# Attention and maxout layer on one core: K and Q through the crossbar one slot earlier, stores held back, queries read in natural order

## The chip, the cores and the metric

The kernel runs on one core of a Trainium2 chip. The metric is the device time of one execution in microseconds (us). Five engines work side by side, each through its own instructions in order: TensorE (PE, with its weight loads shown apart as PEld), VectorE (DVE), ScalarE (ACT), GpSimd (POOL) and SyncE (SP), which here only issues DMA transfers. SP, ACT and POOL each have a queue that can issue DMAs.

## The reference

Sliding-window attention with four sink positions, and on its result a feed-forward layer that takes the largest of three products:

```python
batch, n_heads, seq, head_dim = (4, 8, 768, 64);  n_sink, window = (4, 128)
scores = (1.0 / np.sqrt(D)) * np.matmul(q, k.transpose(0, 1, 3, 2))
keep = (pos[None, :] < n_sink) | ((rel >= 0) & (rel < window))     # rel = query - key
scores = np.where(keep, scores, -1000000000.0)
a = np.exp(scores - max);  a = a / sum(a)
x = np.matmul(a, v).transpose(0, 2, 1, 3).reshape(B * S, H * D)    # 3072 x 512
h = np.maximum(np.maximum(x @ w1, x @ w2), x @ w3)                 # 3072 x 768
out = (h @ w_out).astype(np.float32)                               # 3072 x 512
```

All inputs and the output are float32.

## The kernel before

**Tiling.** The 3072 rows are cut into 12 chunks of 256 rows (`ci`), three for each of the four sequences. A chunk is two blocks of 128 queries. Heads go in four pairs (`p`): the two heads of a pair lie on the two halves of the 128 partitions of the transposed Q and K. The matmuls run in bf16.

**The stages of a chunk.** `load` (L74) brings K, Q and V from DRAM as float32, 512 KB each (L78), with two neighbouring rows on one partition, so that each descriptor moves 512 bytes. Row 2r + i of a block lies on partition r, place i. `cast` (L488) makes bf16 copies of K and Q (`cast_qk`, L173) and of V (`cast_v`, L180), mostly on POOL. K and Q are then transposed so that the head dimension lies on the partitions: in chunks 0 and 1 by float32 matmuls against an identity (`turn32`, L193), in chunks below `KQ_XBAR` = 4 by PE transposes (`turn`, L205), from chunk 4 on by the DMA crossbar on SP (`turn_xbar`, L214: two transposes for K at L217, one for Q at L220). `sink_score` (L248) and `score` (L261) multiply (PE, L254 and L279) and take the exponential (ACT, L258 and L281). `mask` (L283) multiplies by a 0/1 mask on DVE. `av` (L293) multiplies by V, with a column of ones for the sum, and divides on DVE into `x`. `x` is transposed to `xT`: by PE (`xpose`, L328) below `X_XBAR` = 4, by two crossbar transposes on SP (`xpose_xbar`, L337, L339) from chunk 4 on. `ffn_h` (L346) makes one of nine groups of h (eight matmuls of 256 columns, L352): the first of three products is copied by ACT (L356), the two others are taken in by a max on DVE (L358). `F(ci, n)` (L501) is the n-th such group. `ffn_y` (L360) makes one block of y (six matmuls of 512 columns, L363), copies it on ACT (L369) and stores it by two DMAs of 64 rows on SP (L371).

**Permuted queries.** K, Q and V are read from DRAM as "(p i)", so after the transposes the columns are in the order i, r (all even rows, then all odd rows). The score matmuls read Q in that order (`q_ap`, L244). So x, h and y of a block are in the order i, r as well, and the store puts them back with a view of the output as "(r i) f -> i r f", one DMA for each i.

**What sets the order.** The schedule is written out by hand: `manual_schedule` keeps each engine's instructions in program order, and waits are put in where a tile is written or read. Chunks 0 to 3 are written out one by one (L384 to L572), with weight loads on POOL (`load_w`, L144, casting in the DMA) and two loads held back by small writes of POOL into their buffer (`gate`, L69). From chunk 4 on a loop runs (L574 to L594), one slot for each chunk i: `attend(i + 1)` (av and the transposes of x), `cast(i + 2)`, the load of chunk i + 3, four F groups of chunk i, `turn_xbar(i + 2)`, `scores(i + 2)`, the two y blocks of chunk i - 1 with masks between them, and the other five F groups. SP's queue in a slot is then: two transposes of x (i + 1), three loads (i + 3), three transposes of K and Q (i + 2), four stores of y (i - 1).

**Buffers.** Raw loads 3 deep, bf16 K and Q 2, transposed K 4 and Q 3 (`kT`, `qT`, L109), V with ones 4 (`vb`, L111), x, xT and h 3, y 4, exponentials 10, PSUM 8 banks in one rotation (`bank`, L58).

Of the kernel before, what the change touches and what calls it, by code (L numbers as in the profile page):

```python
# [14 lines left out]
def kernel(  # L15
# [17 lines left out]

    nc = tc.nc
# [14 lines left out]
    KQ_XBAR = 4  # L49
    X_XBAR = 4  # L50

    with tc.manual_schedule():
# [21 lines left out]
        def load(ci, parts):  # L74
            b, c = divmod(ci, CPB)
            for t, g in parts:
                h = slice(0, H) if g is None else slice(4 * g, 4 * g + 4)
                nc.sync.dma_start(  # L78
                    out=raws[ci][t][:, h],
                    in_=dram[t][b, h, c * 256:c * 256 + 256].rearrange("h (p i) d -> p h (i d)", i=2))  # L80

        HALVES = [("k", 0), ("q", 0), ("k", 1), ("q", 1), ("v", 0), ("v", 1)]
        for ci in (0, 1):
            load_begin(ci)
            load(ci, HALVES)

# [12 lines left out]
        for i in range(2):  # L99
# [3 lines left out]
                base=-i, pattern=[[1, 2], [2, 64]], channel_multiplier=-2)  # L103
            nc.gpsimd.affine_select(
                out=msk0[ip, 0, 1], in_=msk0[ip, 0, 1], compare_op=ALU.is_gt, fill=0.0,
                base=i, pattern=[[-1, 2], [-2, 64]], channel_multiplier=2)
# [4 lines left out]
        vb = [const.tile([128, 2, H, D + 1], BF16, name=f"vb{s}") for s in range(4)]  # L111
# [17 lines left out]
        def consts_late(eng):  # L129
            for s in range(1, 4):  # L130
                eng.memset(vb[s][:, :, :, D:D + 1], 1.0)
# [48 lines left out]
        def cast_v(ci, n, i, eng):  # L180
            eng.tensor_copy(vb[ci % 4][64 * i:64 * i + 64, n, :, 0:D],  # L181
                            raws[ci]["v"][64 * n:64 * n + 64, :, i])
# [49 lines left out]
        def sink_v(b, eng):  # L232
            t = bank([128, 2, D + 1], F32, "vs_ps")
            for p in range(NP):
                for h in range(2):
                    nc.tensor.matmul(t[32 * p:32 * p + 32, h], lhsT=sel[:, h],
                                     rhs=vb[(CPB * b) % 4][:, 0, 2 * p + h],
# [6 lines left out]
        def q_ap(ci, p, n):  # L244
            x = qT[ci % 3][:, p].rearrange("p i n r -> p n i r")
            return x if n is None else x[:, n]

        def sink_score(ci):  # L248
# [3 lines left out]
            st = bank([128, 2, 2, 64], F32, "sk")  # L252
# [5 lines left out]
            nc.scalar.activation(e, st.rearrange("p n i r -> p n (i r)"), AF.Exp, scale=scale)  # L258
            es[ci, "sink"] = e

        def score(ci, p):  # L261
# [5 lines left out]
            for what in range(lo, 4):  # L267
                if what == 2:
                    continue
                for h in range(2):  # L270
# [4 lines left out]
                    if what == 1:  # L275
                        o = o.rearrange("p n (i r) -> p n i r", r=64)
                    else:
                        o = o.rearrange("p (i r) -> p i r", r=64)
# [14 lines left out]
        def av(ci, pairs, eng=None):  # L293
# [10 lines left out]
            for p in pairs:  # L304
                first = c == 0
                for t in range(2):
                    for s, n in ((2 * t, 2 * c + t - 1), (2 * t + 1, 2 * c + t)):
                        if n < 0:
                            continue
                        for h in range(2):  # L310
                            nc.tensor.matmul(  # L311
                                o[p][:, t, h], lhsT=es[ci, p][:, h, s],
                                rhs=vb[(CPB * b + n // 2) % 4][:, n % 2, 2 * p + h],
# [9 lines left out]
        def xT_of(ci):  # L323
            if ci not in xTs:
                xTs[ci] = work.tile([128, DS, 256], BF16, tag="xT", name="xT")
            return xTs[ci]

        def xpose(ci, g, eng):  # L328
            pt = bank([128, 2, 2, 128], BF16, "xt_ps")
            x = xs[ci].rearrange("p t h d -> p t (h d)")  # L330
            for a in range(2):
                for t in range(2):
                    ds = 2 * g + a
                    nc.tensor.transpose(pt[:, a, t], x[:, t, ds * 128:(ds + 1) * 128], ident)
            eng(xT_of(ci)[:, 2 * g:2 * g + 2], pt.rearrange("p a t c -> p a (t c)"))  # L335

        def xpose_xbar(ci):  # L337
            for t in range(2):
                nc.sync.dma_start_transpose(  # L339
                    out=xT_of(ci)[:, :, t * 128:(t + 1) * 128],  # L340
                    in_=xs[ci][:, t].rearrange("p h d -> p (h d)"))
# [4 lines left out]
        def ffn_h(ci, wi, fp):  # L346
# [3 lines left out]
            for f in range(2):  # L350
                for ds in range(DS):
                    nc.tensor.matmul(hp[:, f], lhsT=w_sb[wi, 2 * fp + f][:, ds],  # L352
                                     rhs=xTs[ci][:, ds], start=(ds == 0), stop=(ds == DS - 1))
# [5 lines left out]

        def ffn_y(ci, t, last=False):  # L360
# [4 lines left out]
            y = work.tile([128, d_model], F32, tag="y", bufs=4, name="y_sb")  # L365
            r0 = ci * 256 + t * 128
            o = out[r0:r0 + 128].rearrange("(r i) f -> i r f", i=2)
            if not last:
                nc.scalar.copy(y, yp)  # L369
                for i in range(2):  # L370
                    nc.sync.dma_start(out=o[i], in_=y[64 * i:64 * i + 64])  # L371
                return
            for i in range(2):
                ip = slice(64 * i, 64 * i + 64)
                if i:
                    nc.vector.tensor_copy(y[ip], yp[ip])
                else:
                    nc.scalar.copy(y[ip], yp[ip])
                (nc.sync, nc.scalar)[i].dma_start(out=o[i], in_=y[ip])

        V, P, A = nc.vector, nc.gpsimd, nc.scalar


        consts_dve()  # L384
        warm(8)
        turn32(0, "k", 0, V.tensor_copy)
        turn32(0, "q", 0, A.copy)
        warm(2)
        score(0, 0)
        turn32(0, "k", 1, V.tensor_copy)  # L390
        score(0, 1)
        turn32(0, "q", 1, A.copy)
        for n in range(2):
            for i in range(2):
                cast_v(0, n, i, P)
        mask(0, 0, V)
        score(0, 2)
        mask(0, 1, V)
        wait_for(raws[1]["k"][0:1, 0, 0, 0:1], P)
        load_w(0, 0, 256)  # L400
        load_w(0, 256, 256)
        load_w(0, 512, 256)
        load_w(1, 0, 256)
        turn32(1, "k", 0, V.tensor_copy)
        score(0, 3)
        turn32(1, "q", 0, V.tensor_copy)
        av(0, [0])
        mask(0, 2, V)
        av(0, [1])
        xpose(0, 0, A.copy)  # L410
        mask(0, 3, V)
        av(0, [2])
        turn32(1, "k", 1, V.tensor_copy)
        av(0, [3])
        turn32(1, "q", 1, V.tensor_copy)
        score(1, 0)
# [10 lines left out]
        mask(1, 0, V)  # L427
        ffn_h(0, 0, 0)
        score(1, 1)
        mask(1, 1, V)  # L430
# [4 lines left out]
        mask(1, 2, V)  # L435
# [3 lines left out]
        mask(1, 3, V)  # L439
        ffn_h(0, 1, 0)  # L440
        av(1, [2, 3])
        ffn_h(0, 1, 1)
        xpose(1, 0, A.copy)
        xpose(1, 1, A.copy)
        ffn_h(0, 1, 2)

        load_begin(2)
        wait_for(wts[2, 0][0:1, 0, 0:1], P)
        gate(2, "kqv", P)
        load(2, [("k", None), ("q", None), ("v", None)])  # L450
        for a in range(2):
            load_wo(a)
        for fp in range(3):
            ffn_h(1, 0, fp)
        cast_qk(2, "k", 0, P)
        cast_qk(2, "k", 1, P)
        for fp in range(3):
            ffn_h(1, 1, fp)
        for i in range(2):
            for n in range(2):  # L460
                cast_v(2, n, i, P)
        ffn_h(0, 2, 0)
        ffn_h(0, 2, 1)
        ffn_h(0, 2, 2)
# [170 lines left out]
```

## Time and profile before

| what | us |
|---|---|
| median of 3 runs (lowest, highest) | 271.96 (270.34, 273.59) |
| the profiled execution | 271.53 |
| its span, first to last instruction | 269.6 |
| one period of the loop, by the chain | 25 to 27 |
| mean granted clock of TensorE | 0.870 of full |

How to read it: the page has the busy time of each engine, the span in 40 slices (a digit is the busy share in tenths; PEclk is the clock that TensorE was granted), and the chain of work that ended last, followed back from the end. A line "A <- B: total, times, longest" in the waits says how long A stood still until B was done. Further lines of the page, the groups of DMA issues with their size and the median time from issue to landing:

```profile
out_dram<-y_sb SPq DMA_DIRECT2D x47, 128.0 KB, 2.4
k_raw<-in_k_dram SPq DMA_DIRECT2D x10, 512.0 KB, 4.6
q_raw<-in_q_dram SPq DMA_DIRECT2D x10, 512.0 KB, 5.8
v_raw<-in_v_dram SPq DMA_DIRECT2D x10, 512.0 KB, 7.1
```

### The profile page before, as it was taken

To read this page: it belongs to the slowest core of one execution; us is meant where nothing else is said; L and a number is where in the kernel's file an instruction comes from. 1 tells how busy PE (TensorE), PEld (TensorE's weight loads), DVE (VectorE), ACT (ScalarE), POOL (GpSimd) and SP (SyncE) were. 2 spreads that over 40 slices of the span, in tenths; PEclk is the share of its full clock that TensorE was granted. 3 is DMA by queue.
4 is the path that set the end of the run, shared out by engine and by line. 5 is a ranking of instruction groups with operands and counts; after the bars stand their busy time and mean duration, and the time that the engine had idled before them with its cause. 6 is when DMAs were issued, how large, how long until landed. Compare 5 with 4: busy or idle time off the path is not lost.

```text
span 269.6 us, 4874 instructions
## 1 busy us (share of the span) xinstructions
PE 186.8 (69%) x1934; PEld 138.2 (51%) x1946; DVE 115.1 (43%) x251; ACT 90.8 (34%) x177; POOL 64.3 (24%) x130
## 2 busy tenths in 40 slices
PE   6878999987777605940894099219903990999992
PEld 5665786774565503830483058115802580587870
DVE  4385676458186502640273028113800380283441
ACT  1528308453727105210711081015202510812221
POOL 3592223647351033005200510070015000000000
PEclk9999999999999965995599579757975798699998
DMA  6999974999892293339033903692187116034133
GB/s 185 278 147 189 199 178 122 251 264 245 216 232 43 47 254 50 80 67 282 4 78 82 270 2 78 162 190 48 38 197 148 45 40 113 0 80 93 26 78 79
DMA packets 71750, 34.92 MB, mean 130 GB/s; under 512 B 27440, under 2 KB 68656, under 8 KB 71728
## 3 DMA queue, kind: packets, MB, share of 16 engines
q1 hardware_dynamic: 67152, 31.34, 52.3%
q0 software_dynamic: 4496, 3.15, 8.1%
q8 instruction: 15, 0.25, 0.4%
q10 hardware_dynamic: 80, 0.13, 0.2%
q14 instruction: 7, 0.06, 0.1%
HBM read 25.17 MB, written 6.29 MB: 117 GB/s over the span
## 4 chain that ended last, share of the span: by engine, by line
PE 54%; DMA 25%; SPq 6%; DVE 5%; ACT 5%; issue 3%; POOL 1%; ACTq 0%; DVEq 0%; POOLq 0%
PE h_ps L352 27%; DMA q_raw<-in_q_dram 14%; PE y_ps L363 13%; DMA qT<-q_bf 10%; PE st L279 5%; SPq L339 4%; PE o_ps L311 3%; ACT e_sb L281 3%; PE kt L200 2%; PE qt L200 2%; DVE e_sb L287 2%; DVE h_sb L358 1%; DMA k_raw<-in_k_dram 1%; SPq L78 1%; SPq L217 1%
## 5 line engine op out<-in xcount | busy, mean ns | idle before, releaser
L352 PE MATMUL h_ps<-xT,w 128*128 128x256 bf16 x864 | 99.1, 273 | 1.2 <-ACT xT L335 1.1
L352 PEld LDWEIGHTS <-w 128*128 128x128 bf16 x864 | 83.5, 98 | 13.4 <-issue 2.1
L358 DVE TENSOR_TENSOR h_sb<-h_sb,h_ps 128x512 bf16<-128x512 bf16 x72 | 49.4, 686 | 54.8 <-PE h_ps L352 47.2
L281 ACT ACTIVATE e_sb<-st 128x512 bf16<-128x512 f32 (+1 forms) x96 | 45.6, 586 | 27.3 <-PE st L279 26.9
L287 DVE TENSOR_TENSOR e_sb<-e_sb,msk 128x1024 bf16<-128x1024 bf16 x32 | 21.8, 696 | 58.1 <-ACT e_sb L281 58.0
L356 ACT CAST h_sb<-h_ps 128x512 bf16<-128x512 f32 x36 | 21.2, 593 | 66.6 <-PE h_ps L352 66.6
L363 PE MATMUL y_ps<-wo,h_sb 128*128 128x512 bf16 x132 | 39.4, 438 | 1.8 <-issue 1.3
L178 POOL CAST k_bf<-k_raw 128x512 bf16<-128x512 f32 x20 | 11.9, 622 | 112.8 <-DMA k_raw<-in_k_dram 97.4
L181 POOL CAST vb<-v_raw 64x512 bf16<-64x512 f32 x48 | 30.5, 636 | 18.3 <-DMA v_raw<-in_v_dram 16.3
L279 PE MATMUL st<-qT,kT 64*128 64x128 bf16 (+1 forms) x256 | 17.7, 293 | 24.1 <-DMA qT<-q_bf 22.2
L254 PE MATMUL sk<-qT,ks 128*32 128x256 bf16 x32 | 2.8, 335 | 42.7 <-DMA qT<-q_bf 42.5
L363 PEld LDWEIGHTS <-h_sb 128*128 128x128 bf16 x144 | 15.2, 112 | 21.9 <-issue 11.9
L279 PEld LDWEIGHTS <-kT 64*128 64x128 bf16 x256 | 11.8, 117 | 28.4 <-issue 26.2
L254 PEld LDWEIGHTS <-ks 128*32 128x32 bf16 x32 | 1.1, 96 | 44.8 <-issue 42.9
L318 DVE TENSOR_TENSOR x_sb<-o_ps,rc 128x256 bf16<-128x256 f32 x48 | 20.4, 424 | 1.6
L369 ACT COPY y_sb<-y_ps 128x512 f32<-128x512 f32 x23 | 13.6, 601 | 17.7 <-PE y_ps L363 13.2
L311 PE MATMUL o_ps<-vb,e_sb 128*128 128x65 bf16 x352 | 14.9, 194 | 3.3 <-DVE e_sb L287 2.8
L258 ACT ACTIVATE e_sink<-sk 128x256 bf16<-128x256 f32 x8 | 3.1, 385 | 41.6 <-PE sk L254 41.6
L311 PEld LDWEIGHTS <-e_sb 128*128 128x128 bf16 x352 | 12.4, 97 | 5.7 <-DVE e_sb L287 3.9
L178 POOL CAST q_bf<-q_raw 128x512 bf16<-128x512 f32 x18 | 10.8, 629 | 6.4 <-DMA q_raw<-in_q_dram 6.4
L289 DVE TENSOR_TENSOR e_sb<-e_sb,msk 128x768 bf16<-128x768 bf16 x16 | 10.1, 651 | 4.6 <-ACT e_sb L281 4.6
L228 DVE COPY ks<-kT 64x16 bf16<-64x16 bf16 x8 | 2.1, 256 | 20.0 <-DMA kT<-k_bf 19.9
(59 smaller groups left out, 79.5 us busy)
## 6 DMA issues: line engine op xcount, KB each, us to landing
out_dram<-y_sb SPq DMA_DIRECT2D x47, 128.0 KB, 2.4
k_raw<-in_k_dram SPq DMA_DIRECT2D x10, 512.0 KB, 4.6
q_raw<-in_q_dram SPq DMA_DIRECT2D x10, 512.0 KB, 5.8
v_raw<-in_v_dram SPq DMA_DIRECT2D x10, 512.0 KB, 7.1
w<-in_moe_w_dram POOLq DMA_DIRECT2D x5, 256.0 KB, 5.6
k_raw<-in_k_dram SPq DMA_DIRECT2D x4, 256.0 KB, 5.2
q_raw<-in_q_dram SPq DMA_DIRECT2D x4, 256.0 KB, 5.3
v_raw<-in_v_dram SPq DMA_DIRECT2D x4, 256.0 KB, 5.4
```

Source lines behind the costliest of these rows:

```text
L178: eng.tensor_copy(bfs[ci, t][:, :, i], x)
L181: eng.tensor_copy(vb[ci % 4][64 * i:64 * i + 64, n, :, 0:D], raws[ci]["v"][64 * n:64 * n + 64, :, i])
L279: nc.tensor.matmul(o, lhsT=kk, rhs=qq, start=True, stop=True)
L281: nc.scalar.activation(e[:, h, lo:], st[h][:, lo:], AF.Exp, scale=scale)
L287: eng.tensor_mul(e, e, msk)
L311: nc.tensor.matmul(o[p][:, t, h], lhsT=es[ci, p][:, h, s], rhs=vb[(CPB * b + n // 2) % 4][:, n % 2, 2 * p + h], start=first, stop=(s == 2 ...
L318: nc.vector.tensor_mul(xs[ci][:, :, 2 * p:2 * p + 2], o[p][:, :, :, 0:D], rc.unsqueeze(3).to_broadcast([128, 2, 2, D]))
L352: nc.tensor.matmul(hp[:, f], lhsT=w_sb[wi, 2 * fp + f][:, ds], rhs=xTs[ci][:, ds], start=(ds == 0), stop=(ds == DS - 1))
L356: nc.scalar.copy(dst, hp)
L358: nc.vector.tensor_max(dst, dst, hp)
L363: nc.tensor.matmul(yp, lhsT=hs[ci][:, fb, t * 128:(t + 1) * 128], rhs=wo[fb // 3][:, fb % 3], start=(fb == 0), stop=(fb == FB - 1))
L369: nc.scalar.copy(y, yp)
```

## The change

Four things are changed together.

1. **Order.** In the loop the casts move from chunk i + 2 to i + 3, the loads from i + 3 to i + 4, and the transposes of K and Q from i + 2 to i + 3; on SP they come directly behind the loads, before the F groups. The scores stay at i + 2. The loop begins at slot 5; slots 2 to 4 are written out. The crossbar takes K, Q and x from chunk 5 on, PE those of chunk 4 too. V gets a fifth buffer.
2. **Stores.** y stays in SBUF (8 chunk-sized tiles); the stores of chunks 0 to 9 are issued on POOL in slots 7 to 11, those of chunk 10 and the first block of chunk 11 on SP, and the last block's by halves on SP and ACT.
3. **Natural order.** The score and sink matmuls read Q as "n r i", so that the columns of the scores, and all that follows from them, are in natural order. A block is stored by one DMA of 128 rows. The masks are built for that order. x is transposed by one crossbar transpose, so xT has the blocks outermost, and the h matmuls read it in two runs of 128 columns.
4. **The beginning.** Twelve and three warm-up matmuls instead of eight and two; the loads of the first two chunks go K, Q, V, V, K, Q by halves, with two of chunk 0 on ACT's queue; the first weights are issued before the second half of V is cast and no longer wait for chunk 1; the load of chunk 2 is released by the weight w2 (index 1, first part) instead of w3's, and the load of chunk 3 by the cast of K of chunk 2.

The diff, cut to its core:

```diff
-    KQ_XBAR = 4
-    X_XBAR = 4
+    KQ_XBAR = 5
+    X_XBAR = 5
...
-        HALVES = [("k", 0), ("q", 0), ("k", 1), ("q", 1), ("v", 0), ("v", 1)]
+        HALVES = [("k", 0), ("q", 0), ("v", 0), ("v", 1), ("k", 1), ("q", 1)]
         for ci in (0, 1):
             load_begin(ci)
-            load(ci, HALVES)
+            load(ci, HALVES, {("q", 0): nc.scalar, ("v", 1): nc.scalar} if ci == 0 else None)
...
         def q_ap(ci, p, n):
-            x = qT[ci % 3][:, p].rearrange("p i n r -> p n i r")
+            x = qT[ci % 3][:, p].rearrange("p i n r -> p n r i")
             return x if n is None else x[:, n]
...
-                        o = o.rearrange("p n (i r) -> p n i r", r=64)
+                        o = o.rearrange("p n (r i) -> p n r i", i=2)
...
         def xpose_xbar(ci):
-            for t in range(2):
-                nc.sync.dma_start_transpose(
-                    out=xT_of(ci)[:, :, t * 128:(t + 1) * 128],
-                    in_=xs[ci][:, t].rearrange("p h d -> p (h d)"))
+            nc.sync.dma_start_transpose(
+                out=xT_of(ci).rearrange("p t s c -> p (t s) c"),
+                in_=xs[ci].rearrange("p t h d -> p (t h d)"))
...
-                    nc.tensor.matmul(hp[:, f], lhsT=w_sb[wi, 2 * fp + f][:, ds],
-                                     rhs=xTs[ci][:, ds], start=(ds == 0), stop=(ds == DS - 1))
+                    nc.tensor.matmul(hp[:, f].rearrange("p (t c) -> p t c", t=2), lhsT=w_sb[wi, 2 * fp + f][:, ds],
+                                     rhs=xTs[ci][:, :, ds], start=(ds == 0), stop=(ds == DS - 1))
...
             if not last:
                 nc.scalar.copy(y, yp)
-                for i in range(2):
-                    nc.sync.dma_start(out=o[i], in_=y[64 * i:64 * i + 64])
                 return
...
+        def store(ci, t, eng):
+            r0 = ci * 256 + t * 128
+            eng.dma_start(out=out[r0:r0 + 128], in_=ys[ci][:, t])
...
-        warm(8)
+        warm(12)
...
-        wait_for(raws[1]["k"][0:1, 0, 0, 0:1], P)
+        cast_v(0, 0, 0, P)
+        cast_v(0, 0, 1, P)
         load_w(0, 0, 256)
...
-        wait_for(wts[2, 0][0:1, 0, 0:1], P)
+        wait_for(wts[1, 0][0:1, 0, 0:1], P)
...
+        ffn_h(0, 2, 0)
         for fp in range(3):
             ffn_h(1, 0, fp)
...
+        load_all(3, True)
...
-        for i in range(4, NCH):
-            attend(i + 1)
-            if i + 2 < NCH:
-                cast(i + 2)
-            load_all(i + 3)
+        for i in range(5, NCH):
+            A_(i + 1)
+            if i + 1 < NCH:
+                xpose_xbar(i + 1)
+            cast(i + 3)
+            load_all(i + 4)
+            KQ(i + 3)
             for n in range(4):
                 F(i, n)
-            if i + 2 < NCH:
-                turn_xbar(i + 2)
             scores(i + 2)
...
+            if i >= 7:
+                n = min(i - 1, held + 3) if i < NCH - 1 else i - 1
+                stores(range(held, n), P)
+                held = n
...
+        stores(range(held, NCH - 1), nc.sync)
         ffn_y(NCH - 1, 0)
+        store(NCH - 1, 0, nc.sync)
         ffn_y(NCH - 1, 1, last=True)
```

`KQ(ci)` is `turn` for K and Q below `KQ_XBAR` and `turn_xbar` from there on; `A_` is `av` of all pairs; `T` is both halves of `xpose`; the first y blocks of chunk 4 stand before the loop (the loop makes y of i - 1 from slot 6 on).

## The prediction

> **What bounds the kernel now.** I read four views in this order: the page's busy shares and 40 slices (is one engine full, and where not), the table of waits (who stands still, for whom), the chain that ended last (the order of events in one period), and the timelines of single lines (what each step costs at full and at half clock).
>
> ```profile
> PE 186.8 (69%) x1934; PEld 138.2 (51%) x1946; DVE 115.1 (43%) x251; ACT 90.8 (34%) x177; POOL 64.3 (24%) x130
> ...
> PE   6878999987777605940894099219903990999992
> ...
> PEclk9999999999999965995599579757975798699998
> ```
>
> The page's slices: PE is nearly full in slices 1 to 13 (to about 92 us), and from there full and empty slices alternate. The clock that is granted falls to about half wherever PE has just been empty, so an idle stretch is paid twice.
>
> ```profile
> PE sk L254 <- DMA qT<-q_bf: 42.5, 6, 11.6
> ...
> PE st L279 <- DMA qT<-q_bf: 22.2, 2, 11.4
> ```
>
> The waits: 64.7 us (42.5 + 22.2) in which PE stood still for the transposed Q of a chunk, 8 times, up to 11.6 us each.
>
> ```profile
> SPq L371 <- ACT y_sb L369: 62.2, 14, 8.0
> SPq L339 <- DVE x_sb L318: 39.3, 8, 6.3
> ```
>
> The waits of SP's own queue, which works strictly in order: it stood 62.2 us before stores of y that weren't ready, and 39.3 us before x. Everything behind them (the loads, the crossbar transposes) stood too.
>
> ```profile
> 141.15 2.63 PE h_ps L352 x24
> 143.78 0.24 SPq L339
> 144.08 1.26 SPq L339
> 145.39 0.58 SPq L78
> 146.02 5.57 DMA q_raw<-in_q_dram
> 151.64 0.16 POOL q_bf L178
> 151.80 3.34 DMA qT<-q_bf
> 155.28 0.41 PE sk L254 x3
> 155.68 1.82 PE st L279 x24
> ```
>
> The chain over one period (they repeat every 25 to 27 us): x is transposed, only then do the loads go out, the Q that arrives is cast, transposed, and PE scores it at once. Load, cast and transpose of one chunk lie end to end inside the same slot, and PE has only four F groups (3.5 us) to put beside them.
>
> ```profile
> 42.03 0.29 PE L254 MATMUL sk<-qT,ks 128*32 128x256 bf16 x4 [0.23 <-ACT qT L191]
> 42.26 1.06 PE L279 MATMUL st<-qT,kT 64*128 64x128 bf16 x24
> ```
> ```profile
> 30.00:56.00 26.00, 25.57 (x266) 20.12 (x268) 14.45 (x29) 12.24 (x23) 8.90 (x20) 1.00 0.81 192
> 56.00:92.00 36.00, 28.58 (x361) 21.39 (x359) 23.18 (x52) 17.82 (x36) 15.22 (x24) 1.00 0.89 180
> ```
>
> The PE timeline at full clock, and two stretches of the table of stretches (length, then busy PE, PEld, DVE, ACT, POOL, clock, DMA share, GB/s): the chunk's 24 score matmuls take 1.06 us here and 1.82 us in the chain above at the lower clock. From 30 to 56 us PE idles 0.43 us of 26; so where its data is there, this PE stream runs without gaps at a clock of 1.00.
>
> **The change, part by part.** All sums are against the profiled execution: span 269.6 us, 271.53 us in all, so 1.9 us lie outside the span. It stands 0.4 us under the median of 271.96.
>
> Step 1, K and Q a slot ahead. The load moves to chunk i+4 (from i+3) and the transposes to i+3 (from i+2, with the scores of i+2 unchanged). The 64.7 us of waiting have then a whole slot of PE work as cover. What remains is PE's own work, which I count from rows at full clock, from the end of F(2,4), at 56.0 us in the trace of before. F groups: 85 by 0.874 (40 matmuls in 4.37) = 74.3. y: 10 chunks by 2.53 (0.21 + 2.32) = 25.3. Attention times V: six chunks by 1.33 and the three that begin a sequence by 0.75 = 10.3. Scores: six by 1.28 (0.29 + 0.99) and three by 1.05 = 10.8. PE transposes of K and Q for chunks 3 and 4 (0.55 each) and of x (0.62): 3.4. Sum 124.1. Then the tail, from the last matmul's end at 264.6 to 269.6: 5.0, unchanged in kind. 56.0 + 124.1 + 5.0 = 185.1. A check by the other road: 269.6 less 64.7 less what the half clock costs a period (score and sink 0.87, y 0.4 to 1.3: say 1.7 by 7 periods, 12) = 193, with the gaps that the first road leaves out.
>
> Step 2, gaps that stay. The stretch 30 to 56 idles at 1.7%, which makes 2 us over 124. The stretch 66 to 92 idles 5.5 us of 26, of which some 3 are waits for the crossbar, and 2.3 for VectorE, whose masks, max and x stand in one order: that rate makes 11. Steady slots are like the first, those of chunks 2 to 4 like the second; I take 6 (2 to 11).
>
> Step 3, the queues. SP lost four stores a slot (about 0.6 us each, but 62.2 us of standing), one of two x transposes, and gains nothing: in a slot x 1.26, three loads 0.58 + 0.57 + 1.12, two kT and one qT at about 1.26 each, 7.3 us of the 13.1 us of PE work in a slot. What stands behind what: x of i+1 waits for VectorE at a slot's start, behind it the loads, and behind them kT and qT of i+3, which nobody needs before the next slot's scores. The added wait (K and Q for the cast) has the next x behind it, and the casts' data should be there some 3 us before the slot begins. The data itself: k, q, v land 6.9 us after the issue of the first at most when alone, and the transposes of a slot move 0.79 MB at some 200 GB/s, 4 us. About 10 us of 13.1, so there is cover, of 3 us, no more. The stores are put off to slots 7 to 11, on POOL: 20 issues at the price of the weight loads' issue on POOL (four in 3.14, 0.79 each) = 15.8 us, on an engine that has no work after 209 us in the trace of before. In slots 7 and 8 six each stand before the casts of the next chunk, 4.7 us; casts take 5.0 of a slot, so the cover is 3 us. Their traffic (half a MB at some 205 GB/s, 2.6 us a chunk, 7.7 a slot) meets load 11 and K and Q of chunk 10: 10 + 7.7 is 4.6 us over the slot. With the slack of 3 in front of it, 2 us reach PE (0 to 8; a gain is excluded, as the same bytes move). The last stores stay on SP and ACT, at the old price. The fifth V buffer and the eight y tiles cost only space.
>
> Step 4, Q read in natural order. Score and sink matmuls now take their moving columns alternately from two places 128 bytes apart, where they took runs of 64 neighbours. No row of the trace shows such a read on PE. Lower end: nothing, at 1.06 us a chunk. Upper end: the same matmuls when columns come half as fast, the rows at the lower clock: 1.82 less 1.06 and 0.40 less 0.29, 0.87 us a chunk; for a chunk that begins a sequence 1.47 less 0.84, 0.63. Chunks 2 to 11: 7 by 0.87 + 3 by 0.63 = 8.0 us. A gain has no source: the columns are as many. I take the upper end, as these rows are the nearest to a moving stream that arrives slowly, and PE has no cover left once it is the bound. [...]
>
> Step 5, the beginning. Twelve warm-up matmuls for eight, Q's first half on ACT's queue, V before the second halves of K and Q, weights before the cast of the rest of V, and the load of chunk 2 released by an earlier weight. At best the first transposes run at full clock: 1.98 + 1.72 against 1.02 + 1.05, a gain of 1.6. At worst the 4.8 us in which POOL waited for the third weight moves on to PE, since weights and chunks 1 and 2 now share the DMA (its share was 1.11 from 10 to 30 us), and F(0,2,0), which needs that weight, is brought forward; in the trace it was there at 27.0 and PE arrives there at about 31, a cover of 4. I take +1 (-2 to +4).
>
> Step 6, the rest, at nothing: x by one transpose for two (Q's transpose is of that shape and lands in 3.1 to 3.4 us, and has a slot), xT read in two runs of 128, the masks' new pattern (made once on POOL before 3 us), one store of 128 rows for two of 64 (same bytes and rows of 2 KB). Their cover is the same slot of PE work; without it, the transpose would cost its 3.4 us a slot.
>
> Sum of the span: 185.1 + 6 + 2 + 8 + 1 = 202.1; with 1.9 outside, 204.0 us.
>
> **The rivals.**
>
> A: the natural-order read costs nothing. For it: the reads in runs of 64 go at 44 ns a matmul (1.06 us by 24), so leaving a run every 64 columns isn't seen; against it: no row leaves its run with each column. 202.1 - 8 + 1.9 = 196.
>
> B: the transfers stay the bound, one slot further on. For it: the cover in a slot is only 3 us, and in 48 to 72 us, where loads, transposes and stores met, two kT issues took 5.40 us where they take 2.5 alone. Against it: the DMA share of the late periods is 0.51 to 0.54, so half of the time is free there. If all of the seven steady slots go at 16.9 us (10 us of transfers and the 6.9 of one load laid end to end) and not at 13.1, it adds 3.8 by 7 = 27: 231, or some 217 if half of them do.
>
> C: that the change doesn't do what it says: K and Q go out a slot early in the program, but the SP queue stands before x so long that they go out no earlier. In the trace SP stood 39.3 us for x, in 8 waits. If each steady slot kept half of its 11 us wait, 7 by 5.5 = 39 us and a cold clock (12): 255. Against it: x waits for VectorE in that slot's first 3 us, and K and Q are not needed in it.
>
> D, the other side: the interleaved read is not twice but many times slower. The scores and sinks of ten chunks cost 7 by 1.28 and 3 by 0.8, 11.4 us at full clock; the gain without step 4 is 271.5 - 196 = 75.5, so it decides from a factor of 1 + 75.5 / 11.4 = 7.6, at which the time is 272; at 10 it would be 299. Against it: no row shows any engine slowed that much by a pattern.
>
> **How the numbers follow.** Forecast (step 4 at about its upper end, the rest as taken) 0.45; A 0.23; B 0.25; C 0.04; D 0.03. The forecast's own range is 197 to 211, from the bounds of steps 2, 3 and 5 taken together in part. The range that is to hold 8 in 10 goes from 193 (A with the gaps at their lower end, 4 less) to 221 (B up to the half of the slots and a little more); C, D, the rest of B and the low end of A lie outside. A difference under 1% is about what a measurement of this kernel can't tell from no change. Forecast, A, B and nearly all of C are faster by over 1%: 0.95; within 1%: 0.02, from the worst of C and the edge of D; slower: 0.03, D.
>
> **What would show it.** Step 1: the waits of PE for qT (64.7 us) gone from the table, the slices full to the end, the granted clock 0.95 or more from 56 us on, a period of 13 to 15 us. Step 2: PE's idle time put down to VectorE or ScalarE, 2 to 11 us. Step 3: SP's waits for y gone; PE idle for qT or xT only in the slots of the first held stores. Step 4: 24 score matmuls in 1.06 us or in 1.8 at a clock of 1.00; this row alone parts forecast and A. Step 5: the first F group at 20 to 25 us, F(2,4) done at 54 to 60. I am wrong if the periods stay over 16 us, with PE waiting for transposes (B, C), or if score matmuls take several us a chunk at full clock (D).

## The result, and the profile after

The changed kernel takes 202.95 us (median of four runs, 201.94 to 204.67) against 272.39 us for the kernel before (four runs, 270.34 to 273.59): a ratio of 0.746 [0.739, 0.754]. The profiled execution took 202.07 us with a span of 200.3, so 1.8 us lie outside it. The four runs lie in two pairs (201.94 and 202.07, 203.83 and 204.67); the views here are of a run of the shorter pair, and a profiled execution that took 205.37 us is shown further down.

The page of the changed kernel, busy shares and the two slice rows that answer to those of before:

```profile
PE 186.8 (93%) x1963; PEld 136.9 (68%) x1975; DVE 115.4 (58%) x250; ACT 93.6 (47%) x182; POOL 76.3 (38%) x156
...
PE   6999989899997999999979999999999999999990
...
PEclk9999999999999999999999999999999999999997
```

PE is busy for as long as before (186.8 us), but in a span that is 69 us shorter: the holes are gone, and with them the half clock behind each hole (mean granted clock 0.993, 0.870 before).

The changed kernel's table of waits (total, times, longest), first TensorE's, then that of SP's own queue:

```profile
PE sk L256 <- DMA qT<-q_bf: 0.3, 1, 0.3
```
```profile
SPq L340 <- DVE x_sb L320: 53.4, 7, 24.7
...
SPq L382 <- ACT y_sb L372: 19.1, 3, 12.9
```

The 64.7 us in which PE stood for qT have become 0.3. SP itself still stands 72.5 us for x and y (101.5 before), longer than before for x, and in this execution hardly anything waits for what is behind. The 19.1 us before y are those of the last stores, after the loop's transfers are done.

PE's timeline over one slot of the changed kernel and the start of the next (start, length, then the group):

```profile
118.95 0.43 PE L256 MATMUL sk<-qT,ks 128*32 128x256 bf16 x4
119.31 2.12 PE L281 MATMUL st<-qT,kT 64*128 64x128 bf16 x24
121.37 2.76 PE L366 MATMUL y_ps<-wo,h_sb 128*128 128x512 bf16 x11
123.97 4.53 PE L353 MATMUL h_ps<-xT,w 128*128 128x256 bf16 x40
...
133.24 0.26 PE L238 MATMUL vs_ps<-vb,sel 128*32 128x65 bf16 x8
...
146.71 0.43 PE L256 MATMUL sk<-qT,ks 128*32 128x256 bf16 x4 [0.34 <-DMA qT<-q_bf]
```

The period is 14.3 us (118.95 to 133.24) where it was 25 to 27. The 24 score matmuls of a chunk take 2.12 us, twice the 1.06 of before, and the next stretches show that this is at a clock of 1.00 (the columns: length, busy PE, PEld, DVE, ACT, POOL, clock, DMA share, GB/s):

```profile
56.00:92.00 36.00, 33.38 (x382) 24.05 (x382) 22.12 (x47) 21.02 (x41) 14.67 (x24) 1.00 0.43 102
92.00:106.00 14.00, 12.72 (x129) 9.19 (x128) 10.18 (x27) 6.00 (x13) 5.82 (x8) 1.00 0.66 170
106.00:120.00 14.00, 14.00 (x167) 10.69 (x166) 9.83 (x20) 6.94 (x14) 5.01 (x8) 1.00 0.88 190
```

From 106 us on PE has no gap worth a name (0.65 us in the 84 to 190). What idles lies from 56 to 106 us: 2.62 and 1.28 us.

So the time went from PE's waits, as the prediction said. Two questions were left: which of the four things that changed together is worth what, and what the read in natural order really costs.

### The profile page after: what moved, and what is told of

Same layout as the page of the kernel before. It is cut to its first block, busy times and chain, and to the rows that moved or that the text cites. A ratio compares the mean times of both kernels' runs of the same rounds, so it can differ in the third digit from the quotient of the medians.

```text
span 200.3 us, 4880 instructions
## 1 busy us (share of the span) xinstructions
PE 186.8 (93%) x1963; PEld 136.9 (68%) x1975; DVE 115.4 (58%) x250; ACT 93.6 (47%) x182; POOL 76.3 (38%) x156
## 4 chain that ended last, share of the span: by engine, by line
PE 71%; DVE 10%; issue 6%; ACT 6%; DMA 4%; POOL 2%; DVEq 0%; ACTq 0%
PE h_ps L353 36%; PE y_ps L366 13%; PE st L281 9%; PE o_ps L313 5%; ACT e_sb L283 3%; DVE h_sb L359 3%; DVE x_sb L320 2%; DMA qT<-q_bf 2%; PE kt L202 2%; DMA k_raw<-in_k_dram 2%; PE sk L256 2%; ACT qT L193 1%; DVE e_sb L291 1%; PE xt_ps L336 1%; POOL out_dram L382 1%
## 5 line engine op out<-in xcount | busy, mean ns | idle before, releaser
L353 PEld LDWEIGHTS <-w 128*128 128x128 bf16 x864 | 83.1, 98 | 13.8 <-issue 2.5
L180 POOL CAST k_bf<-k_raw 128x512 bf16<-128x512 f32 x20 | 12.8, 663 | 66.5 <-DMA k_raw<-in_k_dram 53.3
L366 PE MATMUL y_ps<-wo,h_sb 128*128 128x512 bf16 x132 | 32.9, 380 | 1.9 <-DVE h_sb L359 1.2
L289 DVE TENSOR_TENSOR e_sb<-e_sb,msk 128x1024 bf16<-128x1024 bf16 x32 | 22.6, 711 | 14.8 <-ACT e_sb L283 14.7
L366 PEld LDWEIGHTS <-h_sb 128*128 128x128 bf16 x144 | 13.3, 98 | 17.3 <-DVE h_sb L359 2.1
L281 PE MATMUL st<-qT,kT 64*128 64x128 bf16 (+1 forms) x256 | 24.1, 327 | 0.3 <-ACT qT L193 0.2
L372 ACT COPY y_sb<-y_ps 128x512 f32<-128x512 f32 x23 | 13.5, 622 | 19.1 <-PE y_ps L366 19.0
L382 POOL DMA_DIRECT2D out_dram<-y_sb x20 | 10.8, 545 | 25.9 <-ACT y_sb L372 25.9
L291 DVE TENSOR_TENSOR e_sb<-e_sb,msk 128x768 bf16<-128x768 bf16 x16 | 10.6, 673 | 4.6 <-ACT e_sb L283 4.6
L180 POOL CAST q_bf<-q_raw 128x512 bf16<-128x512 f32 x18 | 12.2, 701 | 0.9 <-DMA q_raw<-in_q_dram 0.9
L319 DVE RECIPROCAL rc<-o_ps 128x4 f32<-128x4 f32 x48 | 8.4, 174 | 4.9 <-PE o_ps L313 4.9
L337 ACT COPY xT<-xt_ps 128x512 bf16<-128x512 bf16 x10 | 5.7, 594 | 8.7 <-PE xt_ps L336 8.7
L202 PE MATMUL kt<-id,k_raw 128*64 128x128 f32 x64 | 5.3, 316 | 0.5 <-DMA k_raw<-in_k_dram 0.5
```

What stands on the lines that cost most here:

```text
L180: eng.tensor_copy(bfs[ci, t][:, :, i], x)
L281: nc.tensor.matmul(o, lhsT=kk, rhs=qq, start=True, stop=True)
L289: eng.tensor_mul(e, e, msk)
L353: nc.tensor.matmul(hp[:, f].rearrange("p (t c) -> p t c", t=2), lhsT=w_sb[wi, 2 * fp + f][:, ds], rhs=xTs[ci][:, :, ds], start=(ds == 0), ...
L366: nc.tensor.matmul(yp, lhsT=hs[ci][:, fb, t * 128:(t + 1) * 128], rhs=wo[fb // 3][:, fb % 3], start=(fb == 0), stop=(fb == FB - 1))
```

## The experiments

In all of them "the lead" is the move of casts, loads and crossbar transposes by a slot. Ratios are to the kernel before on the same chip.

### The lead taken back

```diff
-            cast(i + 3)
-            load_all(i + 4)
-            KQ(i + 3)
+            cast(i + 2)
+            load_all(i + 3)
             for n in range(4):
                 F(i, n)
+            KQ(i + 2)
```

and the same in the slots that are written out, for chunks 6 to 11; all else as in the changed kernel.

> The changed kernel with casts, loads and the K and Q transposes of chunks 6 to 11 back at the offsets of before (cast i+2, load i+3, transposes of i+2 behind the four F groups of the same slot); the stores stay held on POOL and the natural order stays. My theory: the lead is the gain; six slots wait 9 to 11.6 us for qT again and lose 1 to 2 us to the lower clock: 255 to 272. Rival, that the stores in SP's queue were the cause: SP has no stores here, so 203 to 215.

Measured: 260.33 us, 0.952 [0.944, 0.959]. Its waits, TensorE's:

```profile
PE sk L256 <- DMA qT<-q_bf: 32.8, 4, 9.8
...
PE st L281 <- DMA qT<-q_bf: 19.1, 2, 10.1
```

Of eight waits, the six of the chunks whose lead was taken back are there again, 51.9 us in all, and the mean clock is at 0.884. So the lead is worth 57 us here. This kernel is still 13.2 us under the one before on the same chip (273.55), and its waits for qT are 12.8 us shorter (64.7 less 51.9). Only 2.2 us of that are the two waits that stay away, of chunks 4 and 5 (1.38 and 0.78 in the kernel before), whose place in the slots before the loop this run leaves as changed. The other 10.6 us come from the six that are back: each is 1.3 to 2.4 us shorter than it was. Their chain has one transpose of x where the kernel before has two, and in the chain at chunk 8 Q lands in 5.0 us (5.6 before) and its transpose in 2.9 (3.3); what does that was not tried apart.

### The stores alone

The kernel before, with its stores gathered and issued on POOL from slot 6 on (sixteen y tiles), nothing else changed:

```diff
-                    nc.sync.dma_start(out=o[i], in_=y[64 * i:64 * i + 64])
+                    late.append((o[i], y[64 * i:64 * i + 64]))
...
+            if i >= 6:
+                flush(12, P)
```

> The kernel before with only its stores taken off SP: 16 y tiles, and from slot 6 on 12 stores a slot on POOL (64 rows each, as before), the last ones on SP. The order of loads, casts and transposes stays. My theory: SP's 62 us before y are not what K and Q wait for in the loop, where x, the loads, the casts and the transposes of one chunk lie end to end anyway; only the loads of chunks 4 and 5, which stood behind the first stores, come earlier: 262 to 271. Rival: the stores in SP's queue were the bound; then 205 to 230.

Measured: 271.39 us, 0.997 [0.993, 1.001]: no difference, at the upper end of what was expected. Its waits, TensorE's, and those of SP's queue:

```profile
PE sk L254 <- DMA qT<-q_bf: 41.0, 4, 11.7
...
PE st L279 <- DMA qT<-q_bf: 19.9, 2, 10.7
```
```profile
SPq L339 <- DVE x_sb L318: 107.9, 8, 16.1
```

Of the 62.2 us of standing before y only one wait of 18.7 is left, and 68.6 more came before x (39.3 to 107.9). The queue got free and had nothing to do earlier, because x itself is made late. The largest number in the table of SP's waits was not the bound.

### The changed kernel with its stores at once

```diff
+                store(ci, t, nc.sync)
...
-                stores(range(held, n), P)
```

Each block is stored as soon as it is copied, on SP; nothing is held.

> The changed kernel with each y block stored at once, one DMA on SP behind its copy, nothing held. My theory: K and Q have a slot of lead, so SP's wait for y in the middle of a slot delays nothing that is due in it, and the traffic (10 us of loads and transposes and 2.6 of stores a slot) fits a slot of 14 us barely: 202 to 207. Rival: with stores in its queue SP stands before y as it did before the change (62 us of standing), x and the loads come late, and the time is 215 or more.

Measured: 203.06 us, 0.743 [0.739, 0.747], the same as the changed kernel's 0.746. The waits of SP's queue:

```profile
SPq L383 <- ACT y_sb L372: 58.8, 16, 12.4
SPq L340 <- DVE x_sb L320: 21.5, 6, 6.0
```

SP stands 58.8 us before y again, nearly what it stood in the kernel before, and now it costs nothing that shows in the time, since K and Q have a slot to spare. PE waits for qT 1.8 us once and 0.5 once. So holding the stores as the change does it buys nothing.

### Natural order alone

The kernel before with the masks, the read and the stores of the natural order:

```diff
-            x = qT[ci % 3][:, p].rearrange("p i n r -> p n i r")
+            x = qT[ci % 3][:, p].rearrange("p i n r -> p n r i")
...
-                for i in range(2):
-                    nc.sync.dma_start(out=o[i], in_=y[64 * i:64 * i + 64])
+                nc.sync.dma_start(out=out[r0:r0 + 128], in_=y)
```

> The kernel before with only the natural order: Q read alternately from two places, masks, one store a block on SP. If the read is limited by a rate of its own and not by PE's clock, the eight scores behind an idle stretch at half clock take no longer (1.8 us) and only those of chunks 0 to 3 take 1 us more: 272 to 277. If it takes two PE clocks a column at any clock, those at half clock take 3.6 us and the time is 284 to 290. If one store a block is worth something on SP's queue, up to 3 us less than either.

Measured: 277.66 us, 1.016 [1.009, 1.024]: slower by 1.6%, a little over the 272 to 277 expected. Two score groups of its timeline:

```profile
45.36 2.12 PE L279 MATMUL st<-qT,kT 64*128 64x128 bf16 x24
...
136.09 2.13 PE L279 MATMUL st<-qT,kT 64*128 64x128 bf16 x24
```

The first is in a full stretch, where the kernel before takes 1.06; the second comes behind an 11 us wait, where the kernel before takes 1.89 (at 129.19); the clock is 1.00 at the first and 0.50 at the second. So these 24 matmuls take as long at one clock as at the other (2.12 and 2.13 us), where those that read runs take 1.06 and 1.89. The prediction's upper end came from rows at the lower clock, so it lay a little under the truth.

### Reads in runs again, two ways

First, the score matmuls of the changed kernel read Q in runs of 64, and the exponential writes its bf16 result in natural order:

```diff
-                nc.scalar.activation(e[:, h, lo:], st[h][:, lo:], AF.Exp, scale=scale)
+                nc.scalar.activation(e[:, h, lo:].rearrange("p n (r i) -> p n i r", i=2),
+                                     st[h][:, lo:].rearrange("p n (i r) -> p n i r", i=2), AF.Exp, scale=scale)
```

> The changed kernel with the score and sink matmuls reading Q in runs of 64 again; the exponentials put the columns into natural order as they write (ACT writes with a step of two elements), so x, y and the stores stay as changed. My theory: the read alone makes the score matmuls slow at full clock (24 in 2.06 us after, 1.06 before), and PE is the bound, so 24 take 1.06 us again and the time falls by 10 to 12 us, to 191 to 194. Rival, contention: the matmuls are slower because all engines and DMAs are denser in time; then they stay near 2 us and the time at 203. Rival, ACT: the stepped write makes an exponential take up to twice its 0.53 us; the groups behind the scores then wait, and 3 to 8 us of the gain are lost.

Second, the whole kernel goes back to the old column order, with two stores of 64 rows a block on POOL:

> The changed kernel with the old column order all through: reads in runs of 64, permuted x and y, masks of before, two stores of 64 rows a block (40 issues on POOL for 20). My theory: 191 to 195, as e1, because POOL has room for the issues. Rival: the single store a block is what pays; then 203 or more.

Measured: 198.17 us, 0.726 [0.720, 0.732], and 196.34 us, 0.720 [0.715, 0.725]. Both are faster, and both by less than the rows of the read promise. In the first, a part moves to ScalarE: the same group of exponentials in the changed kernel, then in this one (mean ns behind the comma):

```profile
L283 ACT ACTIVATE e_sb<-st 128x512 bf16<-128x512 f32 x64 | 32.4, 621 | 1.2 <-PE st L281 0.7
```
```profile
L283 ACT ACTIVATE e_sb<-st 128x512 bf16<-128x512 f32 x64 | 39.7, 791 | 0.0
```

PE also waits 2.1 us for qT of chunk 10 there. In the second, too, PE meets late transfers. Its PE timeline at the scores of chunk 10:

```profile
141.83 0.41 PE L256 MATMUL sk<-qT,ks 128*32 128x256 bf16 x4 [3.40 <-DMA qT<-q_bf]
142.17 1.89 PE L281 MATMUL st<-qT,kT 64*128 64x128 bf16 x24
143.99 0.61 PE L366 MATMUL y_ps<-wo,h_sb 128*128 128x512 bf16 x1
144.81 3.59 PE L366 MATMUL y_ps<-wo,h_sb 128*128 128x512 bf16 x10 [0.22 <-issue]
148.24 4.53 PE L353 MATMUL h_ps<-xT,w 128*128 128x256 bf16 x40
```

From 138.43, when PE was ready, to the F group at 148.24 it takes 9.8 us for what takes 4.1 where nothing is late (138.55 to 142.66 in the next kernel but one): 3.4 of waiting and 2.3 behind it, where the clock is lower (0.76 over 134 to 148 us, 1.00 in the 14 us on either side). This is step 3 of the prediction, in its place (K and Q of chunk 10, the slots of the first held stores). The changed kernel lost 0.3 us there in the execution shown above, and 2.6 us in another (shown below).

### The first held stores a slot later

```diff
-            if i >= 7:
+            if i >= 8:
```

once in the changed kernel, once in the old column order of the experiment above.

> The changed kernel with the first held stores in slot 8 (chunks 0 to 2), not in slot 7 where the last load is. My theory: in slot 7 stores, load 11 and the transposes of chunk 10 collide and use up the lead; the trace after shows qT of chunk 10 just 0.34 us late. Without the collision it is there in time: 0 to 1 us faster, 202 to 203.

> e2 (reads in runs of 64, permuted order, two stores a block) with the first held stores in slot 8. My theory: e2 gained 6.6 of the 10 us because PE, being faster, met the collision of slot 7: 3.4 us of waiting for qT of chunk 10 and 2.4 us more at the lower clock behind it. Without the collision 190 to 192. Rival: what e2 lacks is lost to VectorE and ScalarE in every slot; then 195 to 197.

The first is a miss. Its four runs took 205.27, 205.53, 208.76 and 208.98 us (median 207.15); by the two shorter ones the ratio is 0.752 [0.747, 0.757], just slower than the stores at once on the same chip (0.743 [0.739, 0.747]) and not to be told from the changed kernel (0.746 and, further down, 0.751). Only the run of 208.76 us has a profile. POOL's timeline and the chain at that place:

```profile
142.14 6.43 POOL L382 DMA_DIRECT2D out_dram<-y_sb  x12
```
```profile
152.30 13.78 DMA qT<-q_bf
```

POOL issued 12 stores of 256 KB back to back, 3 MB, and qT of chunk 11, issued behind them, took 13.8 us to land (median of the seven: 2.9). PE waited 6.4 us for it. In this run the collision was not avoided, only moved to the next chunk; how long PE waited in the two shorter runs is not known.

The second did what was expected, to 0.3 us: 192.25 us, 0.704 [0.701, 0.707], the best of all versions here and 10.7 us under the changed kernel. Its PE timeline over one period:

```profile
112.73 0.29 PE L256 MATMUL sk<-qT,ks 128*32 128x256 bf16 x4
112.95 1.18 PE L281 MATMUL st<-qT,kT 64*128 64x128 bf16 x24
114.25 2.75 PE L366 MATMUL y_ps<-wo,h_sb 128*128 128x512 bf16 x12
...
126.11 0.26 PE L238 MATMUL vs_ps<-vb,sel 128*32 128x65 bf16 x8
```

No wait for qT is left, and the period is 13.4 us instead of 14.3.

### Why the same delay helped one and not the other

The two kernels differ in the read and in the size of a store. The first, again, with each store of 128 rows as two of 64:

```diff
-            eng.dma_start(out=out[r0:r0 + 128], in_=ys[ci][:, t])
+            for i in range(2):
+                eng.dma_start(out=out[r0 + 64 * i:r0 + 64 * i + 64], in_=ys[ci][64 * i:64 * i + 64, t])
```

> The changed kernel with the first held stores in slot 8, as in the run that was slower (207.15 us), but each store of 128 rows split into two of 64 rows (an issue on GpSimd for each). In that run GpSimd issued 12 stores of 256 KB in 6.43 us, 3 MB; in the old column order with the same hold it issued 12 of 128 KB in 6.29 us, half the bytes in the same time, and K and Q of chunk 11 came in time. Theory: the issue price is what paces GpSimd's stores, so halved stores bring half the bytes a microsecond, and the last crossbar transposes go through: TensorE waits under 2 us for Q of chunk 11 (6.38 before), and the time is 199 to 202 us, under that of the changed kernel. Rival: the halves of the stores do nothing; what spared the old column order was that its slots are a microsecond shorter and that its stores fell elsewhere. Then the wait for Q of chunk 11 stays at 5 to 7 us and the time at 206 to 208.

Measured: 201.51 us, 0.740 [0.734, 0.745], under the version with whole stores (0.752 [0.747, 0.757]). POOL's timeline, and PE's:

```profile
144.51 6.81 POOL L383 DMA_DIRECT2D out_dram<-y_sb  x13
```
```profile
162.11 0.43 PE L256 MATMUL sk<-qT,ks 128*32 128x256 bf16 x4
```

13 issues of half the size in about the time of 12 whole ones; qT of chunk 11 landed in 7.7 us, and PE did not wait for it (0.6 us at another chunk). An issue costs POOL 0.52 to 0.54 us for 128 KB as for 256 KB, so a burst of halves brings half the bytes in the same time. The times bear out that the size of the stores matters here. How much of it is a shorter wait does not follow from 6.4 us against none, since the 6.4 come from one of the two longer runs. Halving is no cure for every order: the old column order with stores from slot 7 on had halves as well, and there the wait was 3.4 us, and ten of them came right before K and Q of chunk 10.

### The lead without held stores

The changed kernel without natural order and without held stores: the old column order, and every block stored at once on SP by two DMAs of 64 rows. The changed kernel ran beside it.

> The order of the changed kernel (lead of a slot, new beginning, five V buffers), without its two other parts: the old column order with reads in runs of 64, and each block stored at once by two DMAs of 64 rows on SP, nothing held. My theory: the lead is the whole gain, the natural order costs some 10 us and holding the stores brings nothing: 190 to 194. Rival: four stores a slot in SP's queue stand before y and eat the lead once PE is faster: 197 or more.

> The changed kernel itself, unaltered, beside the two others on the same chip: 201 to 205. It gives the distance to the one with the lead alone on one chip.

Measured: 195.83 us, 0.720 [0.716, 0.723], a little over what was expected, and 204.20 us, 0.751 [0.747, 0.754], for the changed kernel. The miss has one place in PE's timeline:

```profile
93.62 1.58 PE L281 MATMUL st<-qT,kT 64*128 64x256 bf16 x16 [3.04 <-DMA qT<-q_bf]
95.13 4.86 PE L353 MATMUL h_ps<-xT,w 128*128 128x256 bf16 x24
```

Here SP issued four stores at 84.68, when their y was ready, the transposes of kT and qT of chunk 6 went out behind them at 87.19 and 90.70, and PE waited 3.0 us and ran the next 24 h matmuls in 4.86 us instead of 2.78. So an SP store can cost a wait, once; that is what a held store can win, where its own burst does not take it back (192.25 against 195.83, 0.704 against 0.720).

The profiled execution of the changed kernel took 205.37 us here. Its PE timeline at the scores of chunk 10, where the profile of the result has a wait of 0.34:

```profile
148.57 0.43 PE L256 MATMUL sk<-qT,ks 128*32 128x256 bf16 x4 [2.56 <-DMA qT<-q_bf]
...
150.99 4.23 PE L366 MATMUL y_ps<-wo,h_sb 128*128 128x512 bf16 x12
```

PE waits 2.6 us, and the y block behind it takes 1.5 us longer (4.23 against 2.76); the mean clock of this execution is 0.987, that of the other 0.993. The same program thus pays for the first held stores in one execution and hardly in another.

### The price of a read, by itself

The changed kernel with eight times 32 matmuls added before the last y block, whose results nobody reads. All have 128 rows of weights and 256 moving bf16 columns (the fifth 128); they differ in which columns are read and in what order, and the last group in how the weights are read.

> The changed kernel with eight groups of 32 matmuls put in before the last y block, on zeros as weights and on the output weights as moving columns, with different read patterns; their results are thrown away. Only the time of a matmul counts, 256 columns in each, by the distance of starts at full clock. Neighbouring columns: 109 ns. Alternating between two places 256 bytes apart: 180 to 260 ns, if the read pattern alone is the cause; 109 if it is not. [...] Step of two elements in one stream: 109. [...] Alternating runs of eight: 109. The last group loads its weights with a step of two.

Measured, in the chain of this kernel (start, length):

```profile
198.15 3.49 PE pr L373 x32
201.64 7.78 PE pr L374 x32
209.42 3.49 PE pr L375 x32
212.92 3.62 PE pr L376 x32
216.54 7.25 PE pr L377 x32
223.79 6.03 PE pr L378 x32
229.82 3.49 PE pr L379 x32
233.32 3.49 PE pr L380 x32
```

The clock was 1.00 in all of them but for one stretch, from about 221.5 to 228.3 us, in which it was 0.50 although PE did not stand; why is not shown. The stretch takes in the end of L377 and most of L378 (length, busy PE, clock, DMA share, GB/s; below it PE's timeline on both sides of the change):

```profile
223.90:228.20 4.30, 4.30 (x22) 0.50 0.00 0
228.30:229.80 1.50, 1.50 (x13) 1.00 0.00 0
```
```profile
223.61 4.66 PE L378 MATMUL pr<-wo,dsrc 128*128 128x256 bf16 x21
228.07 1.75 PE L378 MATMUL pr<-wo,dsrc 128*128 128x256 bf16 x11
```

The first 21 matmuls of L378 start within 4.46 us, 213 ns apart; once the clock is back, the starts are 135 to 139 ns apart. Those of L377 are 225 to 228 ns apart at both clocks. The table has the full clock unless it says otherwise.

| line | order of the columns | ns a matmul |
|---|---|---|
| L373 | neighbours | 109 |
| L374 | by turns from two places 256 bytes apart (the change) | 243 |
| L375 | by turns from two places 8 bytes apart, inside 16 bytes | 109 |
| L376 | every second element (4 bytes a step) | 113 |
| L377 | every eighth element (16 bytes a step), 128 columns | 227 (at both clocks) |
| L378 | by turns, in runs of 2 elements | 137 (213 at a clock of 0.50) |
| L379 | by turns, in runs of 8 elements (16 bytes) | 109 |
| L380 | neighbours; the weights are read every second element | 109 |

So it isn't the pattern as such that costs. Among these eight, what is slow is a jump of 16 bytes after each column (L377: 227 ns for 128 columns) and one of 256 bytes after one or two (L374 and L378: 243 and 137); turns inside 16 bytes (L375) and a change of place after eight columns (L379) cost nothing, and steps of 4 bytes (L376) 4%.

## Why the prediction was right

204.0 us was predicted, 202.95 came. The mechanism was right: the waits for qT went, and the read took back part of the gain. That the sum lies within 1% is in part luck, since terms that were off cancel. The terms, against the changed kernel's profile:

**Step 1, the lead: right.** From the end of F(2,4) (57.06) to that of the last matmul (195.46) there are 138.4 us; steps 1 to 4 gave 139.2 for this part (124.1 of work, 6, 2, and the read of nine chunks, 6 by 0.87 and 3 by 0.63). The 124.1 has in it K's and Q's PE transposes of chunk 3, which the changed kernel makes before F(2,4) (0.9 us, 55.20 to 56.09); with them it is 139.3. Two errors cancel in this. PE idles 4.6 us where steps 2 and 3 had 8:

```profile
57.06:195.46 138.40, 133.79 (x1375) 97.81 (x1384) 83.83 (x176) 65.43 (x131) 45.84 (x75) 1.00 0.59 145
```

And the stream itself is over 3 us longer than the 124.1, the read apart: 133.8 and 0.9 less the 7.2 of the read is 127.5. A slot of the best version (192.25 us) takes 13.4 us without a wait, where the rows of step 1 add up to 13.0. The tail is 4.8 (5.0 predicted). Taking the lead back cost 57 us and brought six of the eight waits back (260.33 us).

**Step 2, gaps: mis-sized.** PE idles 4.6 us from 56 to 190 (6 predicted), 3.9 of them before 106 us: 1.4 in chunk 3's attention, where VectorE's masks are late, and 1.2 before y, for VectorE's h.

**Step 3, queues and stores: right in place, and in size between two executions.** The place was as named, K and Q of chunk 10 behind the first held stores. 2 us were taken; PE lost 0.3 us there in the profile of the result and 2.6, with 1.5 more in the y block behind it, in the one of 205.37 us. The issues on POOL were priced too high (0.79 us, measured 0.54). In the variants the wait is 2.1 (the stepped exponential) and 3.4 us (the old order) at the same chunk, and 6.4 at the next (stores from slot 8, one of the longer runs). The bound of 8 held them all.

**Step 4, the read: the upper end was right, though not for the reasons given.** It forecast 0.87 us a chunk. By the slots of the changed kernel and of the best version, from the first sink or vs matmul to the y block, it is 0.90 (2.42 against 1.52) and 0.60 for a chunk that begins a sequence (1.76 against 1.16). As rows of matmuls alone it is more, 1.06 and 0.14 for the sink, but the scores of the best version take 0.2 us more a slot (1.52) than those of the kernel before (1.31, from 42.03 to 43.34); why was not tried. The two reasons that it gave do not hold: the half-clock rows are no bound, since the read takes the same at both clocks (2.12 and 2.13 us), and the places are 256 bytes apart, not 128, as i steps over two by 64 elements of two bytes. And chunks 0 and 1, which it left out, pay too: F(2,4) ends at 57.06 in the changed kernel and at 54.04 in the best version, which has the same beginning but reads runs. Of these 3.0 us some 1.1 are chunk 2's, which was counted. From there to the last matmul the two differ by 7.0 us (138.4 against 131.4), where the forecast for nine chunks was 7.1.

**Step 5, the beginning: wrong sign and out of its range, hidden by other terms.** +1 was taken, with -2 as its lower end. Without the read, F(2,4) ends 2.0 us earlier (54.04 against 56.0), although the 0.9 us of chunk 3's transposes now stand before it: for the same work the gain is 2.9 us. Of it 1.4 to 1.7 us lie before the first F group (18.63, and 18.33 in the other kernel of this column order, against 20.04). The price that was feared, POOL's wait for the third weight moving on to PE, did not come. Gain, transposes and the read of chunks 0 to 2 add up to the +1 by chance.

**The rivals.** A (the read is free, 196) fell on the score rows. The old column order did take 196.34 us, but that kernel reads in runs and lost 5.7 us to the collision. B (transfers stay the bound, 217 to 231) fell: the period is 14.3 us, with a wait in one slot. C (K and Q go out no earlier, 255) fell too, since their waits went; the kernel without the lead shows what they cost. D needed a read 7.6 times as slow; it is about twice.

**What stays open.** Why steps of 16 bytes cost 1.77 ns a column (227 / 128) and the turns between two places only 0.95 (243 / 256) isn't shown by any run, and runs of four elements were not tried. Nor is it shown why the clock fell in the probe while PE was busy, what sets apart the executions in which Q of chunk 10 is late, and what PE waited for in the shorter runs of the changed kernel with stores from slot 8. The four pieces of step 5 were not tried apart.

## What to carry to other kernels

Where an engine is starved by a chain that lies end to end inside one slot, move the chain a slot ahead and price the remaining stream from its rows at full clock; that sum came within 1% of the measured time, though with errors of some 3 us that cancelled. A long wait in a queue's table is a bound only if somebody needs what is behind it: 62.2 us of it could be removed for nothing, and 58.8 put back for nothing once there was a lead (with the faster read, holding the stores did gain 3.6 us). Before a layout is changed to save stores, look at who reads it on the engine that will be the bound, and after every gain look again at the transfers that were late by little. One profile is one execution: a wait of 0.3 us in it was 2.6 us in the next. And look up the clock of each stretch before a row is called a price at full clock.

## What the runs showed of the hardware

- Where TensorE read its moving columns by turns from two places 256 bytes apart, 24 score matmuls took 2.12 us at a clock of 1.00 and 2.13 at 0.50; reads in runs of 64 took 1.06 and 1.89. In the probe, steps of 16 bytes took 227 ns for 128 columns at both clocks. For 256 columns, runs of two elements from two places took 137 ns at full clock and 213 at a clock of 0.50, neighbours 109 at full clock, turns inside 16 bytes 109, every second element 113.
- The granted clock fell to 0.50 for some 6.8 us (221.5 to 228.3 us of the probe) while PE was busy without a gap, in the slow reads.
- Reading weights with a step of two elements cost nothing in the probe (109 ns a matmul, as with neighbours).
- An exponential that writes bf16 with a step of two took 791 ns for 128x512, against 621.
- The crossbar transpose of Q on SP landed late behind a burst of stores from POOL: qT of chunk 11 took 13.8 us from issue to landing behind 12 whole stores (3 MB), 7.7 behind 13 halves, where the medians of the same two runs are 2.9 and 3.0.
